# Two PSUM halves for one: a second product's two accumulators share a bank, and third sets of seven products use the freed one

## The chip, the cores and the metric

The kernel runs on one core of one Trainium2 chip. The metric is the device time of one execution in microseconds (us). TensorE (PE) multiplies matrices and writes to PSUM, eight banks of 2 KB for each of 128 partitions. VectorE (DVE) and ScalarE (ACT) read PSUM and SBUF and do everything element by element. POOL and SP mostly issue DMAs.

## The reference

```
qn = q / (norm(q, axis=1) + 1e-6)          # q, k, v: (4, 6080, 256)
kn = k / (norm(k, axis=1) + 1e-6)
a  = softmax(kn^T @ qn / tau)              # 256 x 256 per batch
x  = (v @ a).reshape(24320, 256)
h  = x @ w_in                              # w_in: 256 x 2048
out = gelu_tanh(h) @ w_out                 # w_out: 2048 x 256
```

## The kernel before, in words

**The attention part, per batch.** The norms run over the tokens, so a batch needs G = q^T k (L248, two matmuls for each 128 tokens, accumulated in one PSUM bank) and the column sums of q squared and k squared. Squares are made by ACT (L193) from bf16 chunks of six rows of 128 tokens; DVE folds six rows to three (`fold`, L224), three to one (`fold_more`), and adds that to an fp32 tile `acc` (L233). At the end of a batch `ss_cols` sums `acc` over the partitions with four fp32 matmuls (L282). `roots` takes the root on POOL, `k_factors` the reciprocal. k's factors lie along the partitions and are wanted as a row on all of them: ACT writes them on a diagonal (`k_row`, L399), and an fp32 matmul with ones spreads it (`k_row_pe`, L406). Then come the tanh form of the softmax and AW = a @ w_in (`aw_part`), so that v goes straight to h. All this is done for batch b+1 while batch b's tokens are worked on.

**The blocks.** Each batch is cut into 12 blocks of 512 tokens (the last has 448), 48 in all. A block n has two products.

*The first product*, h^T = AW^T v^T, has 16 slices of 128 rows, in 8 pairs. An ordinary pair is four matmuls of 512 columns into two banks (`mm1`, L521) and one gelu of 1024 columns (`gelu`, L531). Two pairs can be made instead as one *set of seven products*: `small` (L597) does the seven products of a fast 2x2 scheme, 14 matmuls of 256 columns, into a pair of banks `qp` and one bank `rb`; `set_step` joins them: cq (ACT, L613) copies `rb` into `qp`; y5 (ACT, L616) copies a part of `qp` to SBUF; ap and ax (DVE, L618, L621) add; Gq, Gr, Gx (ACT, L623, L628, L631) are the gelus. DVE prepares differences of v (`sums_v`) once a block and of AW (`sums_w`) once a batch. `SETS` gives the pairs of the three sets: (1, 2), (5, 6), (4, 7). `sets_of` tells which a block has: batches 0 to 2 have two sets and four ordinary pairs (the first three blocks fewer sets), the 12 blocks of batch 3 have three sets and two ordinary pairs, 0 and 3.

*The second product*, out^T = w_out^T g, is done with seven products too, M1 to M7, eight matmuls of 256 columns each (`product`, L726; A and B are its halves), which need the differences T1 to T4 of g by DVE (`sums_1`, `sums_2`; T2 to T4 in two halves of 1024 columns). Two accumulators of 256 columns have a bank each, "r" and "p" (`BANK`). M1 goes to r, M5 to p; cq keeps M1 in SBUF (ACT, L736), y5 keeps M5; M6 goes to r; ap (DVE, L776) writes r + y5 to p; M7 goes to r; M3 to p, and c12 turns p into the output tile (DVE, L751); ax (L742) adds r and y5 for c22; M4 goes to r, which c21 turns; M2 starts a new p, c11a adds x1 to it, and c11 turns the sum. When all four quarters of a block are turned, SP stores it in four DMAs (L816).

**The banks.** "a" (G, sums, AW's parts), "s" (`rb`), "r" and "p" have one each, and "h" and "b" have two each, for ordinary pairs and `qp`.

**The order** is written out by hand: `ORDER` has a text of steps for a block, `WINDOW` tells which text each of the 48 blocks takes. "w1m5" is product 5 of set 1, "M3B-1" half B of M3 of the block before, "row4" a row of G, "lv", "lt", "lq", "lk" are DMAs (v cast to bf16 in DRAM by POOL, v transposed by SP, q and k by POOL, each held back to the last matmul before it). Every engine runs its instructions in this order and waits by semaphores.

Of the kernel before, what the change touches and what calls it, by code (L numbers as in the profile page):

```python
# [18 lines left out]
def kernel(  # L19
# [32 lines left out]
    accp = ctx.enter_context(tc.tile_pool(name="accp", bufs=1))  # L52
# [42 lines left out]
    def load_one(b, c, which, gate=None):  # L95
        r0, n = chunks_of(b)[c]
        t = qkp.tile([128, 8, 256], BF16, tag="qk"[which])
        src = (q, k)[which]
        after(nc.gpsimd.dma_start(
            out=t[:, 0:n, :],  # L100
            in_=src[b, 0 : R * 128, :].rearrange("(p r) c -> p r c", r=R)[:, r0 : r0 + n, :]), gate)
        if with_rest(b, c):
            after(nc.gpsimd.dma_start(out=t[:REM, n, :], in_=src[b, R * 128 : N, :]), gate)
        qk_tiles.setdefault((b, c), []).append(t)
# [13 lines left out]
    def cast_first(st):  # L118
        for which in range(2):
# [6 lines left out]
            qk_tiles.setdefault((0, 0), []).append(t)  # L126
# [40 lines left out]
    G, SS, ACC, SQ, SQR = {}, {}, {}, {}, {}  # L167
# [59 lines left out]
    def fold_more(b, c, k):  # L227

        a1 = FOLD[b, c]
        if k == 2:  # L230
            nc.vector.tensor_add(a1[:, 0, :], a1[:, 0, :], a1[:, 1, :])
        elif k == 4:
            nc.vector.tensor_add(ACC[b], ACC[b], a1[:, 0, :])  # L233
        elif b in ACC:
            nc.vector.tensor_add(a1[:, 0, :], a1[:, 0, :], a1[:, 2, :])
        else:
            ACC[b] = accp.tile([128, 512], FP32, tag="acc", name=f"acc{b}")
            nc.vector.tensor_add(ACC[b], a1[:, 0, :], a1[:, 2, :])
# [38 lines left out]

    def ss_cols(b):

        SS[b] = pM.tile([128, 4], FP32, tag="a", name=f"ss{b}")  # L280
        for j in range(4):
            nc.tensor.matmul(SS[b][:, j : j + 1], lhsT=ACC[b][:, j * 128 : j * 128 + 128],  # L282
                             rhs=ones_f[:, 0:1], start=True, stop=True)
# [90 lines left out]
    def norms(b):  # L374
        sv = smx.tile([128, 4], FP32, tag="sv")
        nc.vector.tensor_copy(sv, SS[b])
        NRM[b] = sv

# [15 lines left out]
    def k_row(b):  # L394

        rr, rh = NRM[b]
        dg = smx.tile([128, 256], FP32, tag="lnk", name=f"dg{b}")
        for ic in range(2):
            nc.scalar.activation(dg[:, ic * 128 : ic * 128 + 128], ident, AF.Copy,  # L399
                                 scale=rr[:, 2 + ic : 3 + ic])  # L400
        NRM[b] = (dg, rh)

    def k_row_pe(b):
        dg, rh = NRM[b]
        ps = pM.tile([128, 256], FP32, tag="a", name=f"rk{b}")
        nc.tensor.matmul(ps, lhsT=ones_f, rhs=dg, start=True, stop=True)  # L406
        NRM[b] = (ps, rh)
# [91 lines left out]
    SIDE = ({0: 0, 2: 0, 4: 0, 6: 0}, {0: 0, 3: 0, 5: 0, 7: 0}, {0: 0, 3: 0, 5: 0}, {0: 0, 5: 0, 3: 0})  # L499
    R_BANK = ("", "s", "ss", "sas")  # L500
    WIDTH = [0, 0]

    def pair_of_banks(n, p, name):

        return pH.tile([128, 2, 512], FP32, tag="hb"[SIDE[sets_of(n)].get(p, 1)], name=name)

    def sets_of(n):

        return (0, 0, 1)[n] if n < 3 else 3 if n // NB == B - 1 else 2

    def mm1(n, p):
# [5 lines left out]
        WIDTH[SIDE[sets_of(n)].get(p, 1)] = cols  # L517
# [22 lines left out]
    def sums_w(b, i):  # L540
        if i == 2:
            SW[b, i] = sqp.tile([128, 4, 256], BF16, tag="sq", name=f"sw{b}_2")
        elif (b, 0) not in SW:
            sw = swp.tile([128, 2, 4, 256], BF16, tag="sw", name=f"sw{b}")
            SW[b, 0], SW[b, 1] = sw[:, 0], sw[:, 1]
# [22 lines left out]

    def small(n, i, m):
# [13 lines left out]
        if m == 1:  # L583
            RB[n, i] = pM.tile([128, 512], FP32, tag=R_BANK[sets_of(n)][i], name=f"rb{n}_{i}")
        dst = {2: 0, 3: 1, 5: 1}
        acc = qp(n, i)[:, dst[m]] if m in dst else RB[n, i]
        side = SIDE[sets_of(n)].get(pa, 1)
# [102 lines left out]
    def sums_2(n, i, half):  # L690
# [5 lines left out]
        f0, f1 = half * 4, half * 4 + 4  # L696
# [9 lines left out]
    BANK = {1: "r", 6: "r", 7: "r", 4: "r", 5: "p", 3: "p", 2: "p"}  # L706

    def product(n, i, halves=(0, 1), bank=None):
# [3 lines left out]
        acc = bank or BANK[i]  # L712
        for half in halves:
            first = i in (1, 5, 2) and (n, i) not in HALVES
            HALVES.setdefault((n, i), []).append(half)
            if first:
                ACCS[n, acc] = pM.tile([128, BLK // 2], FP32, tag=acc, name=f"{acc}{n}_{i}")
# [44 lines left out]
    def mm2_step(n, what):  # L762
# [3 lines left out]
        if what[0] == "M":  # L766
            product(n, int(what[1]), (" AB".index(what[2]) - 1,),
                    "s" if last and what[1] == "2" else None)
        elif what == "cq":
            keep(n, "r", "x1")  # L770
# [4 lines left out]
        elif what == "ap":  # L775
            nc.vector.tensor_add(ACCS[n, "p"][:, :hc], ACCS[n, "r"][:, :hc], XS[n, "y5"][:, :hc])  # L776
        elif what == "ax":
            add_out(n, "r", "y5", 1, 1)
# [8 lines left out]
        else:  # L787
            ci, tj = {"c22": (1, 1), "c11": (0, 0), "c12": (0, 1), "c21": (1, 0)}[what]
            if (n, ci, tj) in CS:
                src = CS.pop((n, ci, tj))  # L790
            else:
                src = ACCS[n, {"c12": "p", "c21": "r"}[what]]
# [28 lines left out]
    with tc.manual_schedule():  # L821
# [63 lines left out]
        for f0, f1 in ((0, 256), (256, 512), (512, 1024), (1024, 1536), (1536, 2048)):  # L885
# [14 lines left out]
            "gc": g_copy, "ss": ss_cols, "sv": norms, "pow": roots, "kf": k_factors, "kr": k_row,  # L900
            "krp": k_row_pe, "rsum": row_sums, "rs": row_factors,
# [13 lines left out]
        def step(what, n):  # L915
# [14 lines left out]
            elif what[0] == "T":  # L930
                sums_2(n, int(what[1]), "ab".index(what[2]))
# [4 lines left out]
            elif what in ("qsq", "ksq"):  # L936
                square(b, c, "qk".index(what[0]), "act")
            elif what == "f1":
                fold(b, c)
            elif what in ("f2", "f3", "f4"):  # L940
                fold_more(b, c, int(what[1]))
            elif what == "vtp":
# [26 lines left out]
        for n in range(NN):  # L969
            for x in ORDER[WINDOW[n]].split():  # L970
# [4 lines left out]
WINDOW = [  # L975
    0, 1, 2, 3, 4, 5, 6, 7, 8, 9, 10, 11, 12, 13, 14, 15, 16, 17, 18, 19, 20, 21, 22, 23,
    24, 25, 26, 27, 28, 17, 18, 19, 20, 29, 30, 31, 32, 33, 34, 35, 36, 37, 38, 38, 39,
    40, 41, 42,
]
ORDER = [  # L980
    """g0 lv+3 aw3 G0 aw2 g1 ac2 ac3 aw4 G1 aw5 lq+1 ac4 g2 ac5 g3 G2 aw6 G3 g4 ac6 SW0 aw7 G4 g5
    lk+1 ac7 vtp G5 pA11 g6 vtc0 g7 vtc1 G6 T1a vtq G7""",
    """g0 vtr0-1 vtr1-1 lt+2 lv+3 g1 T2a-1 G0 T2b-1 M1B-1 G1 pF0-1 g2 g3 G2 pS1-1 w0m1+1 pF1-1
    lq+1 M1A-1 G3 g4 cq-1 pS2-1 pNA-1 g5 pS4-1 M6B-1 G5 M5A-1 pS3-1 M6A-1 G4 M5B-1 g7 vs+1
    y5-1 g6 ap-1 G7 T3a-1 lk+1 M3A-1 T3b-1 pA12-1 M7A-1 T4b-1 w0m5+1 M7B-1 w0cq+1 row0 ax-1
    row1 w0y5+1 M3B-1 T4a-1 G6 w0m6+1 M4B-1 c12-1 w0ap+1 M4A-1 qsq M2A-1 c21-1 M2B-1 row2
    c11a-1 M1B ksq T1a w0m2+1 w0m7+1 w0m3+1""",
    """g0 w0Gq T2a-1 lt+2 lv+3 row4-1 M5A-1 w0ax G0 M5B-1 T2b-1 M1A-1 f1-1 g4 cq-1 w0Gx T3a-1
    w0m4 G4 g3 lq+1 f2-1 vs+1 M6A-1 G3 g6 T4b-1 y5-1 M6B-1 c11-2 G6 g5 lt+3 lv+4 ap-1 T3b-1
    w0Gr M3A-1 G5 w0m5+1 T1a w0m1+1 row2 M7A-1 w0cq+1 lk+1 M3B-1 w0y5+1 M7B-1 c12-1 qsq w0m6+1  # L990
    c22-2 g7 w0ap+1 row5-1 T4a-1 row3-1 G7 w0m2+1 ax-1 w0m3+1 w0m7+1 f3-1 M2A-1 ksq M2B-1 T2a""",
    """g0 w0ax w0Gq row5-1 T2b-1 M4A-2 vs+1 M4B-2 G0 w0m4 g4 c21-2 w0Gr c11a-2 f1-1 g3 G4 SW1-3
    M1B-1 lq+1 G3 M5A-1 c22-2 M1A-1 f2-1 w0Gx w1m1 T3b-1 w1m5 M5B-1 w1cq T3a-1 g7 cq-1 T4a-1
    w1y5 lt+3 lv+4 row0-1 w1m6 y5-1 M6A-1 G7 w1ap M6B-1 row1-1 qsq ap-1 w1m2 w1m7 w1m3 w1ax
    row4-1 lk+1 M3A-1 T1a M7A-1 w1Gq w1m4 row3 M7B-1 w1Gr c11-2 M3B-1 f3-1 w1Gx row1 c12-1
    w0m1+1 w0m5+1 T4b-1 row2 w0cq+1 M2B-1 ax-1 M2A-1 w0y5+1 row3-1 ksq c11a-1 w0m6+1""",
    """g0 T3a-1 w0ap M4A-2 G0 M4B-2 T2b-1 M5B-1 T2a-1 w0m7 g3 c21-2 w0ax M1A-1 G3 f4-2 row0-1
    w0m4 M1B-1 c22-2 lq+1 w0Gr T3b-1 w0m3 w0m2 cq-1 w1m5 c11-2 M5A-1 w0Gq f1-1 M6B-1 w1m1 y5-1
    M6A-1 f2-1 w1cq g4 ap-1 lt+3 lv+4 w1y5 T4a-1 w1m6 G4 row4-1 w1ap M3A-1 M7A-1 vs+1 w0Gx
    M3B-1 ksq w1m7 f3-1 lk+1 w1m3 w1ax g7 T4b-1 M7B-1 G7 c12-1 w1m4 row1 ax-1 w1m2 f4-1 M2B-1  # L1000
    w1Gr w0m5+1 w1Gq T1a M2A-1 w0m1+1 M4A-1 w0cq+1 c11a-1 M4B-1 w0y5+1 T2a row5-1 w0m6+1 w1Gx
    M5A c21-1 w0ap+1""",
    """g0 qsq-1 T3a-1 M5B-1 T2b-1 w0m2 G0 M1A-1 f1-1 w0m7 M1B-1 y5-1 w0m3 w0ax cq-1 g3 w0Gq T4b-1
    M6A-1 lq+1 T3b-1 G3 w0m4 g4 vs+1 w0Gr M6B-1 G4 w1m5 ap-1 w1m1 row3-1 f2-1 lt+3 lv+4 row4-1
    w1cq M3A-1 M3B-1 w1y5 w1m6 w0Gx g7 w1ap ksq c12-1 lk+1 row2 w1m2 c22-2 w1m7 w1m3 w1ax
    M2A-1 G7 M7A-1 T4a-1 w1m4 row2-1 f3-1 row0-1 w1Gr M7B-1 T1a w1Gq row5-1 w0m1+1 w0m5+1
    M2B-1 ax-1 w0cq+1 c11-2""",
    """g0 w1Gx-1 T3a-1 w0y5 M4B-2 c11a-2 row0-1 T2b-1 G0 M4A-2 w0m6 c21-2 M5A-1 qsq-1 T2a-1 g3
    w0ap M1A-1 c22-2 M1B-1 f4-2 lq+1 w0m7 cq-1 M5B-1 w0ax G3 row3-1 M6B-1 T4b-1 M6A-1 y5-1
    c11-2 w0m2 w0Gx w0m4 T4a-1 row4-1 w0Gr row1-1 ap-1 w1m5 lt+3 lv+4 w0m3 T3b-1 w1y5 row5-1  # L1010
    w1m1 M3B-1 f1-1 w1cq M3A-1 w0Gq M7B-1 vs+1 w1m6 M7A-1 lk+1 w1ap g4 ksq ax-1 c12-1 w1m7
# [226 lines left out]
```

## Time and profile before

| | |
|---|---|
| time, median of 3 runs | 696.61 us (696.44 to 696.72) |
| the profiled execution: span, first to last instruction | 695.2 us, about 1.4 below the median of the timed runs |
| granted TensorE clock | 0.998 |
| matmuls | 5501 |
| busy: PE, DVE, ACT, POOL | 97%, 91%, 89%, 11% |
| the span's first matmul starts at, its last at | 7.2 us, 688.9 us |
| DMA landing, median: v cast, v transposed, q, k, store | 4.2, 4.8, 4.9, 5.8, 3.2 us |

A group's row gives line, engine, operation, out<-in, shape and count, then busy us and the mean duration in ns of one, then the engine's idle time just before them and who ended it. A wait's row gives who waited, for whom, us in total, times, and the longest. A row of the timeline gives start and length in us; for several merged instructions (x4) from the first's start to the last's end. A matmul's duration reaches to the end of its results, while the next has long begun: distances between starts tell what one costs.

### The profile page before, as it was taken

The numbers are of one execution on the slowest core, as the hardware profiler recorded it, in microseconds if no ns is written. First come the engines' busy times: TensorE is split into PE (matmuls) and PEld (weight loads), VectorE is DVE, ScalarE is ACT, GpSimd is POOL, SyncE is SP. The second block draws the span as 40 slices with busy tenths as digits, with TensorE's granted clock in tenths as the row PEclk, the third lists the DMA queues.
The fourth block names the chain that finished last, engine by engine and source line by source line (L and its number), as shares of the span: only waits on it lengthen the run. The fifth ranks groups of instructions, "written<-read, shape, count | busy, mean of one in ns | idle before, by whom it ended". The sixth has DMA issues, their size and how long they took to land.

```text
span 695.2 us, 14413 instructions
## 1 busy us (share of the span) xinstructions
PE 677.3 (97%) x5501; PEld 530.7 (76%) x5501; DVE 630.8 (91%) x1245; ACT 616.0 (89%) x894; POOL 73.4 (11%) x135
## 2 busy tenths in 40 slices
PE   3999999999999999999999999999999999999996
PEld 2857787777778777777777777777877888888785
DVE  3579998999998889999999889999999999999996
ACT  5389989999889999999988999999888999999993
POOL 4321101111001001101010100010000000000000
PEclk9999999999999999999999999999999999999999
DMA  9996888897478777747587777593563463453325
GB/s 240 207 269 98 160 141 126 114 150 109 65 144 126 130 120 105 122 80 121 91 138 121 119 120 126 97 141 53 83 99 69 77 103 61 81 103 59 54 39 89
DMA packets 161462, 79.07 MB, mean 114 GB/s; under 512 B 148448, under 2 KB 152160, under 8 KB 160672
## 3 DMA queue, kind: packets, MB, share of 16 engines
q0 software_dynamic: 14448, 39.72, 34.2%
q1 hardware_dynamic: 145696, 37.14, 31.8%
q10 hardware_dynamic: 1248, 1.28, 0.6%
q8 instruction: 43, 0.70, 0.4%
q14 instruction: 27, 0.22, 0.1%
HBM read 78.91 MB, written 36.57 MB: 166 GB/s over the span
## 4 chain that ended last, share of the span: by engine, by line
PE 95%; DMA 4%; DVE 0%; issue 0%; POOL 0%; ACT 0%; DVEq 0%; POOLq 0%
PE r L726 24%; PE h L521 22%; PE p L726 18%; PE rb L597 13%; PE qp L597 10%; PE G L248 5%; DMA t<-in_k_dram 2%; PE awp L461 2%; DMA t<-in_q_dram 1%; PE ss L282 0%; PE ss L275 0%; PE vt_ps L325 0%; PE rk L406 0%; PE warm L370 0%; DVE vT_pe L331 0%
## 5 line engine op out<-in xcount | busy, mean ns | idle before, releaser
L726 PEld LDWEIGHTS <-wcomb 128*128 128x128 bf16 x2688 | 261.9, 98 | 43.5 <-issue 0.2
L531 ACT ACTIVATE g<-h 128x1024 bf16<-128x1024 f32 (+1 forms) x178 | 179.9, 1014 | 16.4 <-PE h L521 13.9
L726 PE MATMUL r<-t,wcomb 128*128 128x256 bf16 (+1 forms) x1152 | 163.6, 272 | 0.1
L521 PE MATMUL h<-vT,aw 128*128 128x512 bf16 (+1 forms) x624 | 158.6, 377 | 0.0
L623 ACT ACTIVATE g<-qp 128x1024 bf16<-128x1024 f32 (+1 forms) x103 | 104.7, 1016 | 7.3 <-PE qp L597 5.8
L726 PE MATMUL p<-g,wcomb 128*128 128x256 bf16 (+1 forms) x760 | 108.0, 272 | 0.0
L521 PEld LDWEIGHTS <-aw 128*128 128x128 bf16 x712 | 69.2, 98 | 49.4 <-DVE aw L364 0.6
L597 PEld LDWEIGHTS <-sw 128*128 128x128 bf16 x824 | 80.2, 98 | 25.5 <-issue 1.3
L193 ACT ACTIVATE sq<-t 128x1536 bf16<-128x1536 bf16 (+4 forms) x59 | 79.2, 1359 | 6.2 <-DMA t<-in_q_dram 6.0
L618 DVE TENSOR_TENSOR qp<-rb,yw 128x512 f32<-128x512 f32 (+1 forms) x103 | 70.8, 688 | 12.3 <-PE rb L597 9.5
L597 PE MATMUL rb<-tv,sw 128*128 128x256 bf16 (+1 forms) x412 | 78.0, 271 | 0.2 <-DVE qp L618 0.2
L621 DVE TENSOR_TENSOR xw<-rb,yw 128x512 f32<-128x512 f32 (+1 forms) x103 | 69.5, 674 | 3.9 <-PE rb L597 2.4
L613 ACT ACTIVATE qp<-rb 128x512 f32<-128x512 f32 (+1 forms) x103 | 59.7, 580 | 11.9 <-PE rb L597 6.8
L597 PEld LDWEIGHTS <-aw 128*128 128x128 bf16 x618 | 60.3, 98 | 12.7 <-issue 0.7
L631 ACT ACTIVATE g<-xw 128x512 bf16<-128x512 f32 (+1 forms) x103 | 63.4, 626 | 1.3 <-DVE xw L621 1.2
L616 ACT ACTIVATE yw<-qp 128x512 f32<-128x512 f32 (+1 forms) x103 | 61.2, 594 | 3.7 <-PE qp L597 1.9
L699 DVE TENSOR_TENSOR t<-g,t 128x1024 bf16<-128x1024 bf16 (+1 forms) x96 | 63.4, 668 | 0.6
L701 DVE TENSOR_TENSOR t<-g 128x1024 bf16<-128x1024 bf16 (+1 forms) x96 | 63.8, 673 | 0.0
L703 DVE TENSOR_TENSOR t<-t,g 128x1024 bf16<-128x1024 bf16 (+1 forms) x96 | 63.6, 669 | 0.0
L628 ACT ACTIVATE g<-rb 128x512 bf16<-128x512 f32 (+1 forms) x103 | 61.2, 596 | 2.2 <-PE rb L597 1.7
L248 PE MATMUL G<-t 128*128 128x256 bf16 (+1 forms) x352 | 60.1, 279 | 0.1
L687 DVE TENSOR_TENSOR t<-g 128x2048 bf16<-128x2048 bf16 (+1 forms) x48 | 57.5, 1197 | 0.0
(137 smaller groups left out, 890.0 us busy)
## 6 DMA issues: line engine op xcount, KB each, us to landing
out_dram<-ot SPq DMA_DIRECT2D x174, 128.0 KB, 3.2
vb<-in_v_dram POOLq DMA_DIRECT2D x41, 256.0 KB, 4.2
t<-in_q_dram POOLq DMA_DIRECT2D x21, 384.0 KB, 4.9
t<-in_k_dram POOLq DMA_DIRECT2D x21, 384.0 KB, 5.8
wst<-in_moe_w_out_dram POOLq DMA_DIRECT2D x2, 1024.0 KB, 11.0
t<-in_q_dram POOLq DMA_DIRECT2D x3, 512.0 KB, 14.4
t<-in_k_dram POOLq DMA_DIRECT2D x3, 512.0 KB, 17.2
out_dram<-ot SPq DMA_DIRECT2D x12, 112.0 KB, 2.6
```

Source lines behind the costliest of these rows:

```text
L193: nc.scalar.activation(o, t[:np_, r, :], AF.Square)
L248: nc.tensor.matmul(G[b][:, jc, :], lhsT=qt[:np_, r, jc * 128 : jc * 128 + 128], rhs=kt[:np_, r, :], start=first and jc == 0, stop=jc == 1, ...
L521: mm = nc.tensor.matmul(hp[:, u, :cols], lhsT=AW[b][:, cc, fc * 128 : fc * 128 + 128], rhs=vt_tiles[n][:, cc, :cols], start=cc == 0, stop= ...
L531: nc.scalar.activation(gs(n)[:, 2 * p : 2 * p + 2, :cols], HP.pop((n, p))[:, :, :cols], AF.Gelu_apprx_tanh)
L597: GATE[0] = nc.tensor.matmul(acc[:, u * hc : u * hc + hc], lhsT=lhs[:, u * 128 : u * 128 + 128], rhs=rhs, start=m in (1, 5) and u == 0, st ...
L618: nc.vector.tensor_add(qp(n, i)[:, 1, :c], RB[n, i][:, :c], YW[n, i][:, :c])
L621: nc.vector.tensor_add(XW[n, i][:, :c], RB[n, i][:, :c], YW.pop((n, i))[:, :c])
L623: nc.scalar.activation(gs(n)[:, 2 * pa : 2 * pa + 2, :c].rearrange("p u (t x) -> p t u x", t=2), QP.pop((n, i))[:, :, :c].rearrange("p t ( ...
L631: nc.scalar.activation(gs(n)[:, 2 * pb : 2 * pb + 2, hc:c], two(XW.pop((n, i))[:, :c]), AF.Gelu_apprx_tanh)
L701: nc.vector.tensor_sub(o, quarter(n, 1, 1, f0, f1), quarter(n, 0, 1, f0, f1))
L703: nc.vector.tensor_sub(o, ts[2][:, f0:f1, :hc], quarter(n, 1, 0, f0, f1))
L726: nc.tensor.matmul(ACCS[n, acc][:, :hc], lhsT=wcomb[:, w, fc, :], rhs=x, start=first and k == 0, stop=k == 3, skip_group_check=True)
```

## The change

- The second product's two accumulators become the halves of one bank "r": `rp[:, 0:256]` and `rp[:, 256:512]`. M1, M2, M3 go to r, M5, M6, M7, M4 to p. cq now copies M1 from r into p, on top of which M6, M7 and M4 are summed; M2 is summed onto M1 in r and c11 turns r itself, so c11a goes; ap writes p + y5 to r, where M3 is added. The last block keeps the old form.
- The freed bank "p" lets `rb` alternate between "s" and "p" (`r_bank`), and 23 blocks of batches 0 to 2 (`THREE`) get the third set. The differences of AW for it are made for every batch.
- T2, T3, T4 are one DVE operation of 2048 columns each.
- `acc` and the fp32 column sums go: after each chunk's fold `sum_parts` sums the one bf16 row by four one-column matmuls, and `add_parts` (DVE, four columns) adds it up.
- Eight of the 24 chunks of k are squared by DVE instead of ACT (`K_DVE`).
- k's factors become a row by two DMAs on SP's queue: to DRAM, and back to all partitions.
- Every block has a text of its own in `ORDER`, and all are new; `WINDOW` goes. Loads of v, q and k stand at other places too.

```diff
-    accp = ctx.enter_context(tc.tile_pool(name="accp", bufs=1))
...
         a1 = FOLD[b, c]
-        if k == 2:
-            nc.vector.tensor_add(a1[:, 0, :], a1[:, 0, :], a1[:, 1, :])
-        elif k == 4:
-            nc.vector.tensor_add(ACC[b], ACC[b], a1[:, 0, :])
-        elif b in ACC:
-            nc.vector.tensor_add(a1[:, 0, :], a1[:, 0, :], a1[:, 2, :])
+        nc.vector.tensor_add(a1[:, 0, :], a1[:, 0, :], a1[:, k - 1, :])
+
+    def sum_parts(b, c):
+
+        SS[b, c] = pM.tile([128, 4], FP32, tag="s", name=f"ss{b}_{c}")
+        for j in range(4):
+            nc.tensor.matmul(SS[b, c][:, j : j + 1], lhsT=FOLD[b, c][:, 0, j * 128 : j * 128 + 128],
+                             rhs=ones_bf[:, 0:1], start=j == 0, stop=j == 3, skip_group_check=True)
+
+    def add_parts(b, c):
+        if b in NRM:
+            nc.vector.tensor_add(NRM[b], NRM[b], SS[b, c])
         else:
-            ACC[b] = accp.tile([128, 512], FP32, tag="acc", name=f"acc{b}")
-            nc.vector.tensor_add(ACC[b], a1[:, 0, :], a1[:, 2, :])
+            NRM[b] = smx.tile([128, 4], FP32, tag="sv", name=f"sv{b}")
+            nc.vector.tensor_copy(NRM[b], SS[b, c])
...
         rr, rh = NRM[b]
-        dg = smx.tile([128, 256], FP32, tag="lnk", name=f"dg{b}")
-        for ic in range(2):
-            nc.scalar.activation(dg[:, ic * 128 : ic * 128 + 128], ident, AF.Copy,
-                                 scale=rr[:, 2 + ic : 3 + ic])
-        NRM[b] = (dg, rh)
...
+        d = dram.tile([1, 256], FP32, tag="rk", name=f"rkd{b}")
+        nc.sync.dma_start(out=d.rearrange("o (c p) -> p (o c)", p=128), in_=rr[:, 2:4])
+        NRM[b] = (d, rh)
+
+    def k_row_in(b):
+        d, rh = NRM[b]
+        rk = smx.tile([128, 256], FP32, tag="lnk", name=f"rk{b}")
+        nc.sync.dma_start(out=rk, in_=d.partition_broadcast(128))
+        NRM[b] = (rk, rh)
...
+    K_DVE = {(1, 0), (1, 1), (1, 2), (1, 3), (1, 4), (2, 1), (2, 5), (3, 5)}
+    THREE = {4, 5, 6, 7, 9, 12, 13, 14, 15, 16, 17, 19, 21, 23, 25, 26, 27, 28, 29, 31, 32, 34, 
+             35}
...
+    def r_bank(n, i):
+        kind = sets_of(n)
+        if kind in (2, 3):
+            return "sp"[(sum(2 + (m in THREE) for m in range(3, n)) + i) % 2]
+        return R_BANK[kind][i]
...
-        f0, f1 = half * 4, half * 4 + 4
+        f0, f1 = (0, 8) if half is None else (half * 4, half * 4 + 4)
...
-    BANK = {1: "r", 6: "r", 7: "r", 4: "r", 5: "p", 3: "p", 2: "p"}
+    BANK = {1: "r", 2: "r", 3: "r", 5: "p", 6: "p", 7: "p", 4: "p"}
+    BANK_LAST = {1: "r", 6: "r", 7: "r", 4: "r", 5: "p", 3: "p", 2: "s"}
...
+                elif i == 1:
+                    rp = pM.tile([128, BLK], FP32, tag="r", name=f"rp{n}")
+                    ACCS[n, "r"], ACCS[n, "p"] = rp[:, 0 : BLK // 2], rp[:, BLK // 2 : BLK]
...
         elif what == "cq":
-            keep(n, "r", "x1")
+            nc.scalar.activation(ACCS[n, "p"][:, :hc], ACCS[n, "r"][:, :hc], AF.Copy)
...
         elif what == "ap":
-            nc.vector.tensor_add(ACCS[n, "p"][:, :hc], ACCS[n, "r"][:, :hc], XS[n, "y5"][:, :hc])
+            nc.vector.tensor_add(ACCS[n, "r"][:, :hc], ACCS[n, "p"][:, :hc], XS[n, "y5"][:, :hc])
         elif what == "ax":
-            add_out(n, "r", "y5", 1, 1)
+            add_out(n, "r" if last else "p", "y5", 1, 1)
...
-                src = ACCS[n, {"c12": "p", "c21": "r"}[what]]
+                src = ACCS[n, {"c11": "r", "c12": "r", "c21": "r" if last else "p"}[what]]
...
         for n in range(NN):
-            for x in ORDER[WINDOW[n]].split():
+            for x in ORDER[n].split():
```

One text of the old order and one of the new, those of block 44 (batch 3), cut after the first steps:

```diff
-    """g0 T1a-1 w2Gr-1 w1m1 G0 M4A-2 c11a-2 w0m5 w0m1 T3a-1 M4B-2 w0cq M5B-1 c21-2 w0y5 w1m5
+    """w0m1 w0m5 w0cq M4A-2 M4B-2 lt+2 c21-2 T1a-1 g3 w2Gx-1 T3-1 w2m4-1 w0y5 lt+1 G3 w0m6 w0ap
```

## The prediction

> **What bounds the kernel now.** I read the page's busy rows and its chain first, then who kept TensorE (PE) waiting, then three stretches, then the timeline for the real price of an instruction.
>
> ```profile
> span 695.2 us, 14413 instructions
> ...
> PE 677.3 (97%) x5501; PEld 530.7 (76%) x5501; DVE 630.8 (91%) x1245; ACT 616.0 (89%) x894; POOL 73.4 (11%) x135
> ...
> PE 95%; DMA 4%; DVE 0%; issue 0%; POOL 0%; ACT 0%; DVEq 0%; POOLq 0%
> ```
>
> The chain that ended last is 95% PE; the 4% of DMA are the first loads and the last store. The waits of PE:
>
> ```profile
> PE G L248 <- ACT first L123: 9.9, 2, 7.2
> PE ss L269 <- DVE a L212: 1.3, 1, 1.3
> PE h L521 <- DVE aw L364: 0.4, 1, 0.4
> PE rb L597 <- DVE qp L618: 0.2, 1, 0.2
> ```
>
> All but the last lie in the first 38 us. So PE hardly waits, and a change pays only by taking matmul columns out, as long as no new wait comes. The granted clock is 1.00. Three stretches (PE, weight loads, DVE, ACT, POOL busy us; clock, DMA):
>
> ```profile
> 250.00:300.00 50.00, 50.00 (x400) 38.99 (x399) 47.13 (x93) 48.04 (x66) 6.13 (x12) 1.00 0.78 121
> 550.00:600.00 50.00, 50.00 (x428) 41.50 (x426) 47.47 (x93) 47.09 (x77) 1.95 (x4) 1.00 0.47 82
> 600.00:650.00 50.00, 49.80 (x426) 41.37 (x424) 47.72 (x93) 47.72 (x77) 1.46 (x3) 1.00 0.43 75
> ```
>
> DVE and ACT are 94 to 96% full. The last two stretches belong to batch 3, which already runs three sets a block: with both helpers at 94 to 95% PE still lost only 0.2 us in 100.
>
> A busy matmul's row (273 ns) hides that matmuls overlap. Prices are the distances between starts:
>
> ```profile
> 625.66 0.38 ACT L736 ACTIVATE x<-r 128x256 f32<-128x256 f32 x1
> ...
> 625.92 0.39 ACT L736 ACTIVATE y<-p 128x256 f32<-128x256 f32 x1
> ...
> 626.15 0.60 PE L726 MATMUL r<-t,wcomb 128*128 128x256 bf16 x4
> 626.19 1.04 ACT L623 ACTIVATE g<-qp 128x1024 bf16<-128x1024 f32 x1
> 626.42 0.70 DVE L618 TENSOR_TENSOR qp<-rb,yw 128x512 f32<-128x512 f32 x1
> ...
> 626.59 0.38 PE L597 MATMUL rb<-tv,aw 128*128 128x256 bf16 x2
> ...
> 627.03 0.68 DVE L701 TENSOR_TENSOR t<-g 128x1024 bf16<-128x1024 bf16 x1
> 627.09 0.63 ACT L628 ACTIVATE g<-rb 128x512 bf16<-128x512 f32 x1
> ```
>
> Four 256-column matmuls take 626.15 to 626.59: 0.11 us each (median over the trace 0.1093; 224 columns 0.0957, 512 columns 0.216, 448 columns 0.189). ACT's 256-column copy costs 0.26 (625.66 to 625.92), its 1024-column gelu 0.90 (626.19 to 627.09); DVE's 512-column add 0.61 (626.42 to 627.03). I call these slots. A slot is the row's duration less about 0.11 on ACT and 0.08 on DVE.
>
> All matmuls of the old program at these slots make 669.9 us. Add 7.2 before the first matmul, about 6 after the last and about 9 in the start phase (first loads, slower first matmuls), and some 3 us of the 695.2 are left: the sum of all stalls after 40 us, 24 of them, most 0.07 to 0.17 us, the longest 0.37.
>
> **The change, part by part.** *PE.* In 23 blocks (21 full, two of 448 columns) the third set replaces two ordinary pairs: 8 matmuls of 512 (8 x 0.216 = 1.728) become 14 of 256 (14 x 0.1093 = 1.530), 0.198 saved; in the short blocks 8 x 0.189 - 14 x 0.0957 = 0.172. Together 21 x 0.198 + 2 x 0.172 = 4.5 us. The fp32 column sums (24 passes of 0.112, L282) go, 2.7; 96 bf16 ones take their place at 0.026 (start to start on L269), 2.5. k's row by PE goes (6 passes of 0.217, L406), 1.3. Sum: -4.5 - 2.7 + 2.5 - 1.3 = **-6.0 us** of PE.
>
> *ACT.* A third set costs cq 0.49, y5 0.49, Gq 0.90, Gr 0.48, Gx 0.52 = 2.89 for two gelus (1.81): +1.08, in 23 blocks +24.6. Eight k squares go to DVE (8 x 1.37 = 11.0), the six L399 go (1.8); cq of the second product is the same copy into PSUM (L613 and L616, to PSUM and SBUF, both have a slot of 0.49). Net +11.8 us.
>
> *DVE.* Two adds a set, 0.61 + 0.60: +27.5; eight squares at the slot of L224, +6.9; sums of weights, sa and f3, +5.3. Gone: 47 c11a (0.33) 15.6; acc (24 x 0.60) 14.4 and the three sv copies 0.2; g's sums in one piece save 2 x 0.60 - 1.13 three times in 47 blocks, 9.4. Net 0.
>
> From 38 us to 689 us ACT has 599 and DVE 612 busy us (sum of the stretches). With 6 us less span (645) ACT stands at 611/645 = 94.7%, DVE at 94.9%: as batch 3 before, which lost next to nothing. So load alone costs 0 to 1 us.
>
> *Hand-overs.* This is the price of the one bank. Each time ACT or DVE reads the bank, PE must be elsewhere until they are done. I counted for each such turn the PE slots that the program's order puts in between, against the end of the last matmul after its slot (0.273 - 0.109 = 0.16), 0.04 to ACT's start, the operations, and 0.04 back to PE (both medians from the trace). Old order: 316 turns in r and p, the least has 0.19 us to spare. New order: 193 turns; 51 have under 0.2 to spare, 11 less than nothing. The worst kind is M1, M5, then y5 and cq, then M2 or M6: 0.16 + 0.04 + 0.26 + 0.38 + 0.04 = 0.89 needed, the median cover 1.09 (eight matmuls cover 0.87). The same turn was cq alone, 0.63 against 1.31. The missing cover sums to 0.6 us if ACT and DVE are free at that moment; the tight waits of before show up to 0.1 more per turn, and that makes 2.2. I take 1.5.
>
> By the Trainium skill, "PSUM — Partial Sum Buffer", section "PSUM bank collisions raise a hardware error", two engines must not be in one bank at a time, whichever columns they use. By it, disjoint halves buy no overlap, and 19 of the new program's waits follow (M7 on c12's transpose, for instance, which reads the other half): at most 19 x 0.36 = 6.9 us by the transposes' slot if uncovered, nothing if covered. No run here shows a shared bank yet.
>
> *k's row by DMA.* DVE's reciprocal to S0/S1 now spans a store of 4-byte pieces and a broadcast load, in turn on SP. The order leaves 5.9 to 7.1 us. No row shows either; from 1.7 each (56 KB stores) to 4.8 + 3.2 (transposes, 128 KB stores), 3.4 to 8.0 us: between no wait and 4.3 us of DVE standing in three places, which PE then feels. The nearest rows are the small stores: 0.5.
>
> *Loads.* vT is asked for later: its first reader comes at least 10.1 us after (27 before), q and k at least 8.0 (13 before). The slowest of before took 9.4 and 8.1; covered, with no reserve.
>
> Sum: -6.0 + 0 + 1.5 + 0.5 = -4.0, and 0.2 for load: span 695.2 - 3.8 = 691.4. The median shown is 1.4 above the span (696.6), so **692.8 us**.
>
> **Rivals.** *The order holds as before*: the turns' waits replace old ones of like size (3 us were lost anyway), 696.6 - 6.0 = 690.6. For it: batch 3's rows; stalls may even shrink a little, 689.7. Chance 0.27. *Forecast*, 691.5 to 695.2: 0.45. *The gain is eaten*: upper ends together, hand-overs 2.2, k's row 4.3, load 1, -6.0 + 7.5 = +1.5, about 698.0; 695.2 to 698.0: 0.14. *Slower*: ACT is inside a gelu when M5 ends, so y5 waits half of 0.90, in each of the 45 blocks after the start: 45 x 0.45 = 20 us less 6.0, 710.6. It decides from 6.0/45 = 0.13 us a block. Against it: the order puts y5 just behind M5, and ACT has 34 us idle; for it: at 95% this idle must fall at the right moments. Chance 0.14. By the bank rule of the Trainium skill ("PSUM — Partial Sum Buffer", the section named above) the same sign comes if none of the 19 is covered: 692.8 + 6.9 = 699.7; it has its place within this case. That third sets don't save their 0.2 us has no chance of its own: batch 3 shows the 0.11 slots.
>
> **How the numbers follow.** The measurement tells 0.2% (1.4 us) from no change. Under 695.2: 0.27 + 0.45 = 0.72; 695.2 to 698.0: 0.14; above: 0.14. The range 690.0 to 698.0 leaves out the 0.14 and about 0.05 below; the likeliest case's own range is 691.5 to 695.2.
>
> **What would show it.** L597 gains 322 matmuls and L521 loses 184; matmul slots sum to about 664; ACT about 94% and DVE about 94% busy; PE's waits in the second product (rp on ACT rp, on DVE rp and ot) a few tenths each. Wrong if PE waits 0.4 us or more on y5/cq block by block, if DVE waits for rk over 1 us, or if the q, k, v loads appear before PE, DVE or ACT.

## The result, and the profile after

The changed kernel takes **744.67 us** (median of 6 runs, 742.1 to 748.84) beside 696.66 before: ratio 1.0699, interval [1.0671, 1.0726]. The forecast was 692.8 with a range up to 698.0: the sign is wrong, and the time lies 46.7 us above the range. The profiled execution took 746.23.

First the page of after: span, busy rows, 40 slices of PE and of its clock, and the chain's shares by engine and by line.

```profile
span 744.1 us, 14684 instructions
...
PE 685.6 (92%) x5637; PEld 546.4 (73%) x5705; DVE 638.0 (86%) x1123; ACT 628.6 (84%) x949; POOL 72.8 (10%) x135
...
PE   4999999997799999699789999999969999999996
...
PEclk9999999999799999899989999999989999999999
...
PE 61%; DMA 16%; ACT 11%; DVE 8%; issue 4%; POOL 0%; DVEq 0%; ACTq 0%; POOLq 0%; SPq 0%
PE rp L736 28%; PE rb L602 11%; PE h L521 9%; PE qp L602 8%; DMA t<-in_k_dram 4%; DMA rkd<-rr 4%; PE G L253 3%; DMA vT<-vb 3%; DMA rk<-rkd 2%; ACT g L628 2%; ACT yw L621 2%; ACT g L531 2%; DMA vb<-in_v_dram 2%; ACT qp L618 1%; DMA t<-in_q_dram 1%
```

The chain was 95% PE; now PE has 61%, DMA 16%, and ACT and DVE 19% together. The DMAs in it are k's row (rkd, rk) and the loads of k, q and v. PE's slices are no longer level: they fall to 6 and 7 in places, and the clock's slices fall with or just behind each of the four stops listed below. The waits of DVE, then of ACT (us in all, times, longest):

```profile
DVE S L403 <- DMA rk<-rkd: 23.4, 3, 8.8
DVE sq L194 <- DMA t<-in_k_dram: 13.4, 4, 7.1
```

```profile
ACT th L408 <- DVE S L403: 22.2, 3, 8.9
...
ACT sq L192 <- DMA t<-in_q_dram: 7.9, 3, 4.1
```

DVE stands for k's row three times, about 8 us each, and ACT stands behind it. In PE's own list the DMAs of k's row do not appear; PE waits for what DVE should have done behind the stop:

```profile
PE rp L736 <- DVE ot L761: 29.6, 5, 8.3
...
PE G L253 <- DMA t<-in_k_dram: 2.3, 2, 1.4
```

The four stretches with such a stop, in after (columns as in the prediction):

```profile
175.00:200.00 25.00, 16.70 (x114) 11.97 (x113) 13.83 (x24) 13.38 (x21) 1.63 (x3) 0.80 0.49 79
300.00:325.00 25.00, 18.07 (x129) 13.41 (x129) 15.63 (x25) 16.07 (x24) 2.63 (x5) 0.86 0.90 145
350.00:375.00 25.00, 17.34 (x148) 14.07 (x148) 16.89 (x35) 17.70 (x27) 1.59 (x2) 0.95 0.67 53
525.00:550.00 25.00, 17.81 (x144) 13.81 (x145) 17.32 (x34) 16.40 (x27) 1.04 (x1) 0.93 0.25 42
```

All three engines are idle for 7 to 12 of the 25 us. I use one measure from here on, the **excess**: a stretch's length less the slots of the matmuls in it, a matmul whose record is missing (5637 of 5705 are there) counted by its weight load. In these four it is 10.98, 8.84, 7.95 and 8.21, 36.0 us together; in the whole span 67.1, where before had 11.9. The stops of PE are 8.2 us at 181.5, 7.66 at 367.1 and 6.69 at 541.3 (k's row) and 6.77 at 303.8 (a load of k). The chain inside the first (start, length, what):

```profile
172.54 9.85 DMA rkd<-rr
...
182.45 5.83 DMA rk<-rkd
...
188.37 0.76 DVE S L403 x2
...
190.13 2.08 PE rp L736 x9
```

The store of 1 KB took 9.85 us and the load behind it 5.83. In the stop at 303.8 the chain has a load of k in the same place:

```profile
294.24 14.80 DMA t<-in_k_dram
```

A second cost shows in the last line of the first chain, where nine matmuls take 2.08 us. PE's timeline just behind that stop, and the stretch to 195.03 (columns as in the prediction):

```profile
190.13 1.86 PE L736 MATMUL rp<-g,wcomb 128*128 128x256 bf16 x8 [8.25 <-DVE ot L761]
191.79 1.91 PE L736 MATMUL rp<-t,wcomb 128*128 128x256 bf16 x8
193.50 1.06 PE L521 MATMUL h<-vT,aw 128*128 128x512 bf16 x2
```

```profile
190.13:195.03 4.90, 4.90 (x20) 2.90 (x20) 4.90 (x6) 3.21 (x5) 0.00 (x0) 0.50 0.83 146
```

Sixteen matmuls from 190.13 to 193.50 are 0.21 each, where the slot is 0.109, and the granted clock is 0.50 until 195.0. Half of these 4.9 us, about 2.5, is lost after the stop is over. Behind the other three stops the clock is 0.50 for 3.5, 4.5 and 5.0 us, which makes 1.7 to 2.5 us a stop. By the Trainium skill, "TensorE: Matmul & The Clock Gate", section "Part 1: The HAM clock gate", PE falls to half its clock after an idle window and needs some microseconds of work to come back; the trace agrees, with these 3.5 to 5.0 us.

The four stretches hold 36.0 of the 67.1. Some 14 of the rest lie in the first 100 us. Most of what is left is in waits too small for such a list, in every block; there the single bank was suspected.

### The profile page after: what moved, and what is told of

It reads as the page before. It is cut to its first block, busy times and chain, and to the rows that moved or that the text cites. A ratio compares the mean times of both kernels' runs of the same rounds, so it can differ in the third digit from the quotient of the medians.

```text
span 744.1 us, 14684 instructions
## 1 busy us (share of the span) xinstructions
PE 685.6 (92%) x5637; PEld 546.4 (73%) x5705; DVE 638.0 (86%) x1123; ACT 628.6 (84%) x949; POOL 72.8 (10%) x135
## 4 chain that ended last, share of the span: by engine, by line
PE 61%; DMA 16%; ACT 11%; DVE 8%; issue 4%; POOL 0%; DVEq 0%; ACTq 0%; POOLq 0%; SPq 0%
PE rp L736 28%; PE rb L602 11%; PE h L521 9%; PE qp L602 8%; DMA t<-in_k_dram 4%; DMA rkd<-rr 4%; PE G L253 3%; DMA vT<-vb 3%; DMA rk<-rkd 2%; ACT g L628 2%; ACT yw L621 2%; ACT g L531 2%; DMA vb<-in_v_dram 2%; ACT qp L618 1%; DMA t<-in_q_dram 1%
## 5 line engine op out<-in xcount | busy, mean ns | idle before, releaser
L736 PE MATMUL rp<-t,wcomb 128*128 128x256 bf16 (+1 forms) x1504 | 209.4, 274 | 8.3 <-DVE ot L761 7.1
L736 PE MATMUL rp<-g,wcomb 128*128 128x256 bf16 (+1 forms) x1128 | 161.8, 275 | 24.7 <-DVE ot L761 22.6
L531 ACT ACTIVATE g<-h 128x1024 bf16<-128x1024 f32 (+1 forms) x132 | 133.3, 1016 | 18.7 <-PE h L521 17.0
L628 ACT ACTIVATE g<-qp 128x1024 bf16<-128x1024 f32 (+1 forms) x126 | 127.1, 1015 | 10.3 <-PE qp L602 9.5
L602 PEld LDWEIGHTS <-sw 128*128 128x128 bf16 x1008 | 98.4, 98 | 25.0 <-issue 3.8
L521 PE MATMUL h<-vT,aw 128*128 128x512 bf16 (+1 forms) x385 | 109.4, 381 | 3.1
L602 PE MATMUL rb<-tv,sw 128*128 128x256 bf16 (+1 forms) x504 | 94.9, 273 | 0.8 <-DVE qp L623 0.2
L618 ACT ACTIVATE qp<-rb 128x512 f32<-128x512 f32 (+1 forms) x126 | 73.4, 583 | 11.4 <-PE rb L602 4.5
L761 DVE STREAM_TRANSPOSE ot<-rp 128x256 f32<-128x256 f32 (+1 forms) x141 | 59.4, 434 | 9.0 <-PE rp L736 7.6
L708 DVE TENSOR_TENSOR t<-t,g 128x2048 bf16<-128x2048 bf16 (+2 forms) x49 | 57.9, 1183 | 0.9 <-ACT g L633 0.4
L704 DVE TENSOR_TENSOR t<-g,t 128x2048 bf16<-128x2048 bf16 (+2 forms) x49 | 57.7, 1178 | 0.9 <-ACT g L636 0.4
## 6 DMA issues: line engine op xcount, KB each, us to landing
wst<-in_moe_w_out_dram POOLq DMA_DIRECT2D x2, 1024.0 KB, 11.9
```

The costliest lines, as they stand in the source:

```text
L521: mm = nc.tensor.matmul(hp[:, u, :cols], lhsT=AW[b][:, cc, fc * 128 : fc * 128 + 128], rhs=vt_tiles[n][:, cc, :cols], start=cc == 0, stop= ...
L531: nc.scalar.activation(gs(n)[:, 2 * p : 2 * p + 2, :cols], HP.pop((n, p))[:, :, :cols], AF.Gelu_apprx_tanh)
L602: GATE[0] = nc.tensor.matmul(acc[:, u * hc : u * hc + hc], lhsT=lhs[:, u * 128 : u * 128 + 128], rhs=rhs, start=m in (1, 5) and u == 0, st ...
L618: nc.scalar.activation(qp(n, i)[:, 0, :c], RB[n, i][:, :c], AF.Copy)
L628: nc.scalar.activation(gs(n)[:, 2 * pa : 2 * pa + 2, :c].rearrange("p u (t x) -> p t u x", t=2), QP.pop((n, i))[:, :, :c].rearrange("p t ( ...
L736: nc.tensor.matmul(ACCS[n, acc][:, :hc], lhsT=wcomb[:, w, fc, :], rhs=x, start=first and k == 0, stop=k == 3, skip_group_check=True)
```

## The experiments

Three parts were to be told apart: k's row, the loads, and what is left when both are mended. T1 is the theory that each costs what its stop shows; T2, that the bank and the order cost most of it.

**k's row back on PE** (e1), otherwise after (its matmul stands 15 to 30 steps later, the steps that use the row 3 to 8):

```diff
-        nc.sync.dma_start(out=d.rearrange("o (c p) -> p (o c)", p=128), in_=rr[:, 2:4])
+        for ic in range(2):
+            nc.scalar.activation(dg[:, ic * 128 : ic * 128 + 128], ident, AF.Copy, scale=rr[:, 2 + ic : 3 + ic])
...
-        nc.sync.dma_start(out=rk, in_=d.partition_broadcast(128))
+        ps = pM.tile([128, 256], FP32, tag="a", name=f"rk{b}")
+        nc.tensor.matmul(ps, lhsT=ones_f, rhs=dg, start=True, stop=True)
```

> The kernel after with one part undone: k's row is made on PE again (two diagonal copies on ACT, one fp32 matmul into bank a, placed just behind the copy of G), nothing goes through DRAM; all else as in the kernel after. Theory 1 (transfers that come late are most of the loss): the three waits of DVE for rk (23.4 us) and PE's excess of 27.1 us over its slots in the three slices where they lie go, about 1.5 us of it stays as in the neighbouring slices, and the row's own work on ACT and PE gives back under 1 us: 718 to 722 us against 744.7. Theory 2 (the hand-overs in the one bank, with ACT and DVE about 95% full, are most of it): the time only moves to other waits, and less than 8 us comes back: over 736.

712.66, ratio 1.0233 [1.0218, 1.0249]: 32.0 us less, 5 beyond T1's range. The three waits, the half-rate stretches behind them and part of the wait for k's load (below) all go. T2 is out for this part.

**Loads of q and k up to 130 steps ahead of their readers**, as their buffers allow (e2; one of k, which stood 270 ahead, goes back), and **both** (e3). One of the moves:

```diff
-    lk+2 (step 1503, batch 2's chunk 7, 73 steps ahead of its reader)
+    lk+3 (step 1445, the same load, 130 steps ahead)
```

> The kernel after with the loads of q and k issued earlier: each goes up in the order to at most 130 steps (some 21 us) ahead of its first use, as far as its buffer is free there, and one k load that took a buffer 270 steps ahead of its use goes back; nothing else moves. Theory 1: DVE's 13.4 us of waits for k and ACT's 7.9 us for q mostly go; the excess of PE in the slice with the longest (8.8 us) falls to about 1, and one or two smaller ones go: 9 to 12 us less, 733 to 736. Theory 2: under 3 us less, over 742.

735.2, 1.0546 [1.052, 1.0573]: 9.5 less, as expected.

> Both edits of the last two runs in one kernel. Theory 1: the savings add, 34 to 38 us less, 707 to 711; what is left above the kernel before (696.7) is then the small waits, about 10 us, and the start. Theory 2: over 733. If the two sorts of wait hide one another, the saving is clearly under or over the sum of the two alone.

708.01, 1.0169 [1.0152, 1.0186]: 36.7 less, as expected, and 4.8 less than the sum of the two parts, since e1 alone already shortened DVE's wait for k from 13.4 to 7.7. So the transfers are 36.7 of the 48.0 us. There remain 11.4 above before and 15.2 above the forecast. e3's stretch from 100 to 675, then the same of before:

```profile
100.00:675.00 575.00, 568.80 (x4748) 460.77 (x4805) 540.01 (x950) 542.34 (x842) 46.29 (x86) 1.00 0.60 100
```

```profile
100.00:675.00 575.00, 574.78 (x4670) 454.24 (x4669) 542.02 (x1079) 533.75 (x792) 47.03 (x87) 1.00 0.63 102
```

The clock is whole again, and PE is idle for 6.2 us in place of 0.2 (part of this is missing records: 4748 matmuls beside 4805 weight loads). By slots the excess from 100 us on is 14.7 beside 2.1.

**Why is the store so slow?** Three stores with other pieces. In e4 each partition's two values lie side by side in DRAM (128 pieces of 8 bytes, not 256 of 4); e5 writes each value twice (256 pieces of 8 bytes, and two more DVE copies); e6 makes two stores (128 pieces of 4 bytes each).

```diff
-        out=d.rearrange("o (c p) -> p (o c)", p=128), in_=rr[:, 2:4]
+        out=d.rearrange("o (p c) -> p (o c)", p=128), in_=rr[:, 2:4]          (e4)
+        out=d.rearrange("o (c p j) -> p (o c) j", p=128, j=2), in_=r2         (e5)
+        for c in range(2): out=d[:, c * 128 : c * 128 + 128].rearrange("o p -> p o"), in_=rr[:, 2 + c : 3 + c]   (e6)
```

> The kernel after with k's row stored in the order in which it lies, 128 pieces of 8 bytes in place of 256 of 4; DVE then reads the row with a step of two elements. If the 8.0 to 9.8 us of the store go with the number of its pieces, each of the three waits falls by 2 to 4 us: 733 to 739 in all. If they are a fixed price of a store and a load one behind the other, or set by other traffic, the time stays within 2 us of 744.7.

> The kernel after with every number of k's row stored twice: still 256 pieces, but of 8 bytes; the row's load then brings 256 KB in place of 128, and DVE has two small copies more. If the price of the store goes with the number of pieces, its landing stays at 8 to 10 us and the time at 743 to 750. If it goes with the size of a piece (4 bytes dear, 8 cheap), the store lands in 3 to 4 us and the time is 712 to 720.

> The kernel after with the store of k's row in two, each of 128 pieces of 4 bytes, one behind the other on SP. If the price goes with the number of pieces of one transfer, each lands in about 3 us (the row of 128 pieces of 8 bytes took 3.0) and the time is 712 to 718. If it goes with the size of a piece, they land in 5 us or more, the second in 8 to 10 when they run one behind the other, and the time is 730 to 747.

Their lines among the DMA issues (count, KB each, median us to landing), of after, e4, e5 and e6 in turn:

```profile
rk<-rkd SPq DMA_DIRECT2D x3, 128.0 KB, 4.9
...
rkd<-rr SPq DMA_DIRECT2D x3, 1.0 KB, 9.7
```

```profile
rkd<-rr SPq DMA_DIRECT2D x3, 1.0 KB, 3.0
```

```profile
rkd<-r SPq DMA_DIRECT2D x3, 2.0 KB, 3.2
```

```profile
rkd<-rr SPq DMA_DIRECT2D x6, 0.5 KB, 7.7
```

e4: 712.05, 1.0232 [1.0207, 1.0257], under both expectations: DVE's wait for rk falls from 23.4 to 2.3, and this edit alone gives back as much as e1. e5: 722.84, 1.0376 [1.0317, 1.0436] (two runs, 719.27 and 726.4), 3 above the range expected if 4-byte pieces are dear: the store lands in 3.2 with as many pieces as after, and DVE waits 5.8, so the number of pieces is not the cause. e6: 750.71, 1.0776 [1.0745, 1.0808], 4 above the range for the same case: half as many 4-byte pieces per store still take 7.7 (7.0 to 16.1), and DVE waits 28.9. The **4-byte piece** is what costs; 8 bytes take a third. Why it does stays open: in the trace of after, the store's 256 packets ran within 0.5 us (173.2 to 173.7), and its end was reported only at 182.39. The Trainium skill ("DMA: Bandwidth & Descriptors", section "Specifications") sets one bound, 512 bytes, below which a write becomes a read-modify-write; 4 and 8 bytes both lie below it, so it does not explain their difference.

**Do the third sets pay?** e8 is e3 with ordinary pairs for the 23 third sets (in each block steps w2... give way to g4 G4 or g7 G7; `rb` and the column sums take banks s and p by a written list).

> The kernel with k's row on PE and the loads early (708.0), and without the 23 third sets that the change brought: their pairs are computed with eight products and two gelus again, put where the set's steps were; the last batch keeps its third sets, the second product its one bank. PE's slots grow by 4.5 us. If the third sets' own hand-overs are what is left (7.2 us of waits in front of matmuls of the sets' banks, 1.9 in the kernel before), 4 to 6 us of waits go and the time stays within 2 us of 708. If the hand-overs in the one bank or the fullness of the order alone are, the waits stay and the time is 711 to 713; if ACT's and DVE's work (23 times about 1.1 and 1.2 us less) was what made everything late, nearly all of the waits go: 700 to 704.

715.02, 1.0266 [1.0249, 1.0283], above all three expectations and 7.0 above e3: the 23 sets save 7.0 where slots say 4.5. The excess from 100 us on is 17 beside e3's 14.7: the small waits stayed with less work on ACT and DVE and without these sets, so neither alone makes them. (Steps were exchanged in e3's order and no new order was sought, which may be the other 2.5.)

**Does the one bank cost anything?** e9 takes all 35 third sets out; e10 does too and puts the two sums of the second product in two banks in the last batch (where `rb` then takes turns with bank a in place of p).

```diff
-                    ACCS[n, "r"], ACCS[n, "p"] = rp[:, 0 : BLK // 2], rp[:, BLK // 2 : BLK]
+                    pp = pM.tile([128, BLK], FP32, tag="p", name=f"pp{n}") if two else rp
+                    ACCS[n, "r"], ACCS[n, "p"] = rp[:, 0 : BLK // 2], pp[:, BLK // 2 : BLK]
```

> No third sets at all, in the last batch neither (35 in place of none go back to eight products), one bank for the second product; the pair of the next run. PE's slots grow by 6.9 us over the 708.0: 713 to 722 by how much the waits change.

> The same with the two sums of the second product in banks of their own in the last batch (11 blocks), and nothing else. If the one bank is what costs (a matmul on one half waits for a read of the other, and the reverse), the stretch of the last batch is 1.5 to 4 us shorter than in the run beside it. If it costs nothing by itself, the two agree within 0.7 us.

720.59 and 719.1 (1.0345 and 1.0324 [1.0303, 1.0344]); spans 717.4 and 716.7. The 0.7 does not come from the batch that differs: slice by slice from 550 to 690 the excess agrees within 0.05 (1.44 and 1.44 from 575, 0.83 and 0.83 from 600); 0.5 of it stands before 80 us. So the shared bank costs nothing here that can be measured. That cq must follow y5, as data, stays in both, and no run parts the bank in an order with third sets.

**Then it is the order.** With the cause left in the steps' sequence, I wrote new sequences for e3's instructions, chosen by the durations and lags that the traces show (PE's end to ACT or DVE 0.20, back to PE 0.05, ACT to DVE 0.03). Only the text of the order differs; 92% of the steps move, by 3 or 4 places in the median, and from e15 on the loads by about 30. The first steps of block 44 (e3, then e18):

```diff
-    w0m1 w0m5 w0cq M4A-2 M4B-2 lt+2 c21-2 T1a-1 g3 w2Gx-1 T3-1 w2m4-1 w0y5 lt+1 G3 w0m6 w0ap M1B-1
+    lt+1 w2Gq-1 w2ax-1 M4B-2 c21-2 g3 w0cq c12-2 w2Gx-1 T1a-1 w1m4-1 w0y5 M1B-1 w0m6 w2m4-1 M1A-1 G3
```

> The kernel with k's row on PE and the loads early (708.0), every instruction kept, only the order of the steps changed (each step by some places up or down, the loads not): chosen so that no matmul comes up before the ACT or DVE instruction that it follows in its bank has had its measured time (0.20 us from PE to ACT or DVE, 0.05 back, and 0.03 us after the end of the one before on ACT or DVE where one must wait for it, in place of 0.10 and 0.08 before that end). If what is left is a matter of the order alone, PE's excess over its slots from 100 us on falls from about 13 us to under 2 and the time is 691 to 695, under the kernel before. If the one bank and the fuller ACT and DVE bound it whatever the order, it stays at 702 or more.

767.49, 1.1038 [1.0999, 1.1078]: a miss. My choice left out that a buffer is written again only behind its last reader. Such places became waits, as in this line of PE's list:

```profile
PE qp L602 <- DVE qp L623: 13.3, 23, 0.9
```

The longest wait, 8.1 us up to 50.5, has another cause: ACT stands behind a load of w_out that comes late.

> Again the kernel with k's row on PE and the loads early (708.0) with every instruction kept and only the order of the steps changed, from the measured durations, but now with the waits that the first new order (767.5) showed and its choice had left out: a buffer is first written again only behind the last reader that stands ahead of it in the order, and a matmul and a read of the other bank of one two-bank tile wait for one another. If what is left above the kernel before is a matter of the order, PE's excess from 100 us on falls from about 13 us to under 3 and the time is 690 to 695, under the kernel before (696.6). If the one bank and the fuller ACT and DVE bound it whatever the order, it stays at 702 or more.

706.16, 1.0155 [1.0127, 1.0182]: with that rule in, the excess from 100 us on falls from 14.7 to 7, but the first 100 us have 17.2, where the loads now come late:

```profile
PE G L253 <- DMA t<-in_k_dram: 6.9, 2, 5.4
```

> The second new order again (706.2; its excess from 100 us on was 7 us in place of 15, but the first 100 us had 17 in place of 12, with one wait of 5.6 us for a load of k), chosen anew with the landings that the loads showed in it, the longest of two runs and 0.8 us more, so that no square or Gram row stands ahead of its load in the first 100 us. If what is left above the kernel before is a matter of order and of loads that come late, the time is 692 to 697. If the one bank and the fuller ACT and DVE bound it, it stays at 702 or more.

> The same choice with 0.03 us of reserve asked for at every hand-over between engines. If the waits that are left come from hand-overs that are met to the hundredth, this one is the faster of the two, by 1 to 3 us; if not, they agree within 1 us. 693 to 698 by the order, 702 or more if the bank or the engines bound it.

708.61, 1.0185 [1.0162, 1.0208] and 708.9, 1.0159 [1.0125, 1.0193]. By the numbers expected, these two and e12 fall on the side of the bank and the full engines (702 or more); the rows say otherwise. The small waits are gone in most stretches (0.1 to 0.4 us per 25), and between 225 and 350 the transfers of v are late instead, in e13:

```profile
DVE tv L558 <- DMA vT<-vb: 8.4, 3, 5.1
```

So the loads have to move with the steps.

> As the third new order (708.6), in which the small waits were gone from 100 to 225 and from 375 us on (0.1 to 0.4 us of excess in 25 us, 0.6 to 0.9 with the old order) and 8 to 13 us went into waits for vT, q and k between 225 and 350: the loads are now moved too, so that every use stands at least 14 us (q, k), 12 (the cast of v) or 10 (vT) behind its load's issue. If the rest is order and late loads, 692 to 697 us. If the one bank and the fuller engines bound it, 702 or more.

> The same rule with another outcome of the search for the order (no reserve asked for at the hand-overs): within 2 us of the run beside it if the leads of the loads are what decided, 692 to 697.

698.18 (10 runs), 1.0024 [1.0014, 1.0033], and 704.35, 1.0111 [1.0097, 1.0125], 1.2 and 7.4 above the range expected. Both follow one rule, loads at least 14 us (q, k) and 10 to 12 us (v) ahead; e16 loses 4.9 us of its difference in one wait at 45.7 us, again behind a late load of w_out, for which ACT waits 5.2.

> The order of 698.2 improved once more, by the landings that its own loads showed in the first 50 us too (it still lost about 12.6 us to waits in the first 100 us, the kernel before 9.6). PE's slots are 4.7 us fewer than before's, the small waits from 100 us on 2 to 4 us more: if the start comes within 1 us of the kernel before's, 694.5 to 697, so the change with its transfers and its order mended comes out at or just under the kernel before; over 698.5 if the start does not mend.

> The same with 0.03 us of reserve asked for at every hand-over: within 1.5 us of the run beside it, 695 to 698.

705.26 (8 runs, 697.45 to 709.36), 1.0103 [1.0071, 1.0136] without the two longest, and **696.17** (11 runs, 695.75 to 697.16), 0.9995 [0.9986, 1.0003]. e17 scatters; in its profiled execution PE lost 5.6 us between 275 and 300, behind a load of k that came late. e18, with 0.03 us in reserve at each hand-over, is level with before. The two were expected within 1.5 us of one another and lie 9.1 apart: which order by the rule comes out well was not foreseen, and e18 is the best of eight. Its page, and its stretch from 100 to 675:

```profile
span 694.0 us, 14701 instructions
...
PE 670.3 (97%) x5641; PEld 543.7 (78%) x5711; DVE 634.9 (91%) x1123; ACT 625.8 (90%) x955; POOL 73.5 (11%) x135
...
PE 89%; DMA 5%; DVE 2%; issue 1%; ACT 1%; POOL 0%; POOLq 0%; SPq 0%; DVEq 0%; ACTq 0%
```

```profile
100.00:675.00 575.00, 571.44 (x4837) 470.18 (x4897) 546.23 (x966) 547.66 (x856) 46.09 (x84) 1.00 0.61 102
```

The same instructions as in e3, in another sequence, loads included, take 11.8 us less.

## Why the prediction was wrong, by its own steps

The 48.0 us between before and after come apart as 36.7 of transfers (after to e3) and 11.8 of order, moved loads included (e3 to e18); e18 stands 0.4 under the runs of before beside it.

| us | before the matmuls | slots | excess | tail | span |
|---|---|---|---|---|---|
| before | 7.2 | 669.9 | 11.9 | 6.2 | 695.2 |
| e18 | 6.9 | 665.2 | 15.4 | 6.6 | 694.0 |

- **PE, -6.0: right, as a sum of slots.** After's slots sum to 663.9, 6.0 under before; e18 has its row of k back on PE (1.3) and is 4.7 under. The third sets' 4.5 is there (e8's slots are 669.7, e3's 665.2), and in time they save 7.0.
- **Load of ACT and DVE, 0 to 1: not contradicted.** ACT is busy 12.6 us more (11.8 forecast). DVE is busy 7.2 more and not 0, probably because more of its instructions wait for the one before them and then no longer overlap it (the lag is given below). In e18 the same work stands with most of the small waits gone, so neither load makes them.
- **"The nearest rows are the small stores: 0.5": the step that failed, with the sign.** The working asked how long a store of 4-byte pieces and a load take, and bounded the pair at 8.0 us by rows whose pieces are far larger. Measured 9.7 and 4.9, 14.6 together; less the 5.9 to 7.1 of the order, about 8 in each of three places, as DVE's 23.4 says. Then PE's half rate, 2.3 to 2.5 behind each of these three stops, and what else a stop delays: 32.0 by e1. The upper bound of 4.3 was no bound, as no row had 4-byte pieces.
- **"Covered, with no reserve": failed, 9.5** by e2, 4.7 on top of e1. The forecast compared the new distances with the slowest landings of before (9.4 and 8.1; a load of q issued at 41 us, which took 10.8 there, was left out). In after the loads are issued at other moments: those of q and k took 7.2 and 6.8 in the median, where before had 4.9 and 5.8. A cover with no reserve is a cost not yet priced.
- **Hand-overs, +1.5, at most 2.2: the mechanism was right, the size was not, and one term was missing.** Excess from 100 us on grew from 2.1 to 14.7 in e3, and e18's order brings it to about 4. In e3 the waits of rp for y5, cq, ap and the output steps come to 5.7 us, those of the sets' banks rb and qp to 7.2 (before 1.9), that for k's row on PE to 1.2. The sum counted the turns in r and p alone; the sets' banks, whose waits grew by 5.3, stood in it at nothing. One lag was left out of the working, as the next lines of ACT in after show:

```profile
464.52 0.38 ACT L746 ACTIVATE y<-rp 128x256 f32<-128x256 f32 x1
464.93 0.37 ACT L782 ACTIVATE rp<-rp 128x256 f32<-128x256 f32 x1
465.21 0.59 ACT L621 ACTIVATE yw<-qp 128x512 f32<-128x512 f32 x1
```

  y5 and cq start 0.41 apart, cq and the next, which needs nothing of it, 0.28. In before two copies of this size, of which neither needs the other, started 0.26 apart. cq copies M1, but writes over M5, which y5 reads; so it takes its place behind y5, and starts 0.03 after y5's end instead of 0.11 before it. That is 0.14 us on the turn that the prediction put at 0.89, against a median cover of 1.09; so many turns with little to spare are over. ACT has about 80 such pairs in before, 150 in after and in e3, and 100 in e18; DVE about 130, 180 and 160. That this lag, rather than the missing reserve as such, makes most of the 11.8 is argued and not shown: no run takes the lag away alone, and the new orders changed both.
- **The rivals.** "The order holds as before" did not come: e3, with its transfers mended, is still 11.4 above before. "Slower" had the right sign by another mechanism: ACT inside a gelu does not show (in e3 PE's waits of rp for y5 and cq come to 3.2, not 20). The bank rule of the Trainium skill ("PSUM — Partial Sum Buffer", section "PSUM bank collisions raise a hardware error") was given at most 6.9; e9 and e10, which differ in such waits in the last batch, show no cost of them. "The gain is eaten" named two of the terms that count, hand-overs and k's row, with upper ends that were too low; its third, the load of ACT and DVE, was not one, and late loads stood in no rival.
- **The signs listed** did their work: "if DVE waits for rk over 1 us" and "if the q, k, v loads appear before PE, DVE or ACT" both came true and named 36.7 of the 48.0.

What stays open: e18 starts worse than before (its excess is 3.5 larger in all, about 1.6 of it in the first 100 us), so the 4.7 us of matmul slots are real and are spent again in the start and in small waits. Whether an order exists that keeps them, no run shows.

## What to carry to other kernels

A transfer whose like is not in the trace, in piece size as much as in bytes, has no upper bound from the trace: measure it alone, or give it a stated reserve. In a kernel whose engines are all 95% full, taking instructions away was worth its slots here only as far as the order was made anew with the real lags, loads included; that was worth 11.8 us, twice what was taken away. A stop of 7 to 8 us on PE should be priced with the half-rate matmuls behind it, here 1.7 to 2.5 us more.

## What the runs showed of the hardware that was not expected

- A 1 KB store of 256 pieces of 4 bytes landed after 9.7 us, 128 pieces of 4 bytes after 7.7 (7.0 to 16.1, two such stores in turn); of 8 bytes, 128 pieces after 3.0 and 256 after 3.2.
- An ACT instruction that waits for the one just before it on ACT starts 0.03 us after its end; without the wait it starts 0.105 before that end: 0.137 lost. On DVE 0.117. The Trainium skill ("VectorE: DVE Perf Modes", section "The DRAIN you can't avoid") says of chained DVE copies that a semaphore after each costs nothing extra; the 0.117 here is the price of waiting for the one before, which that figure does not single out.
- Readers and writers in two halves of one PSUM bank showed no cost over two banks in the last batch of e9 and e10 (0.05 us per 25 us).
